# An attention and soft mixture-of-experts kernel: the w2 of expert 5 loaded whole, joins by single copies, and a first output batch stored in two parts

## The chip, the cores and the metric

The kernel runs on one core of one Trainium2 chip. The metric is the device time of an execution in microseconds (us); the median of several runs is compared. Times inside an execution come from one profiled execution and count from the start of its span.

## The reference

Attention with 8 batches, 8 heads, 576 positions and head size 64 is followed by a soft mixture of experts over all 4,608 rows. Four heads see a window of 32 positions, the other four every fourth position of a window of 128. The output of attention is `x` (4608 x 512).

```
logits = x @ phi                                  # 4608 x 32 slots
d = softmax of logits over the rows               # dispatch
slot_input = (d.T @ x).reshape(8, 4, 512)         # 8 experts, 4 slots each
h = np.maximum(slot_input[e] @ w1[e], 0.0)        # 4 x 1024
slot_out[e] = h @ w2[e]                           # 4 x 512
c = softmax of logits over the slots              # combine
out = c @ slot_out                                # 4608 x 512
```

All inputs and the output are float32 in HBM. The kernel computes in fp16 with float32 sums; its DMAs convert on the way.

## The kernel before, in words

**Attention** (lines 445 to 551) runs over the 8 batches as a pipeline of four stages whose order is written out by hand (`ORDER`, line 48); the scheduler keeps the program order on every engine (line 445). ET holds exp(logits) with the slots on partitions, U the sum of d.T @ x.

**Weights.** All loads, and all stores of the output, are issued by GpSimd (POOL), in program order and into one DMA queue. w1 of all experts and w2 of experts 0 to 2 are loaded during attention. When the buffers of the raw inputs are free, lines 536 to 547 load the rest: w2 of experts 3 and 4 whole (1,024 KB as fp16, one DMA each, line 201); then, for the left 256 columns (`s = 0`) and after them for the right 256 (`s = 1`), w2 of experts 5, 6 and 7. Each such half goes as two DMAs of 256 KB (lines 205 to 207). A DMA uses one of eight semaphores in turn, so each issue also waits until the DMA eight before it has landed.

**Slots** (lines 563 to 613). `rs` takes the row sums; `si` holds the slot inputs of the two halves of heads on 64 partitions. Lines 576 to 586 transpose it to `siT` in PSUM, per half `k` with two transposes, and copy it into the block-diagonal `siTm` (half 0 by DVE, half 1 by ACT). Line 596 multiplies by w1 of all experts (64 matmuls), lines 603 to 613 apply the maximum with zero and bring the result, transposed, into `hTm`.

**Second product and join** (lines 621 to 648). `emit_so(s, experts)` adds the products with w2 into `so` in PSUM, eight matmuls for each expert, over all 512 columns (`s` is None) or one half of them. The rows of `so` hold partial sums in four groups. `gather_so(s)` copies a half of the columns to SBUF (`so_part`), and `spread_so(s)` multiplies it by a matrix of ones that adds the groups and repeats the result for them (`rep`), and copies that to `so_sb`. Each of these copies is done in two parts of 128 columns, one by DVE and one by ACT (`part_cols`).

**Output** (lines 652 to 703). `emit_fin` makes one tile of 128 rows: a matmul of ET with `so_sb` (L654), then the scaling by the row's sum, which is also the eviction from PSUM, by ACT (L663) and DVE (L667) in turn. `emit_batch` makes four of them and stores them with one DMA (L674). The order (lines 679 to 698) is: products of experts 0 to 4 over all columns, left products of 5, 6 and 7, left join; then the left half of six batches, with right products put in before the third (expert 5), the fourth (6) and the sixth (7); the right gather before the sixth and the right spread after it; the right half of these six batches; batches 6 and 7 over all columns; and the last 64 rows of every batch (`om_l`, two stores, L701). Left batch, right batch, left store and so on are counted from 0 where they carry a number; the first right store is R0.

Of the kernel before, what the change touches and what calls it, by code (L numbers as in the profile page):

```python
# [9 lines left out]
FP32 = mybir.dt.float32  # L10
FP16 = mybir.dt.float16
# [6 lines left out]
S = 576  # L18
# [7 lines left out]
E_EXP = 8  # L26
S_PER_E = 4
N_SLOTS = 32
# [12 lines left out]
DH = DMODEL // 2  # L41
# [55 lines left out]
def kernel(  # L97
# [10 lines left out]
    nc = tc.nc  # L108
# [9 lines left out]
    ident = cst[:, o : o + 128]  # L118
    spread = cst[:, o + 128 : o + 256]
# [7 lines left out]
    si = consts.tile([64, 4 * D], FP16, name="si")  # L127
    siTm = consts.tile([128, 4, E_EXP, N_SLOTS], FP16, name="siTm")
    rrow = consts.tile([128, NFIN], FP32, name="rrow")
    so_part = consts.tile([128, DMODEL], FP16, name="so_part")  # L130
    so_sb = consts.tile([128, DMODEL], FP16, name="so_sb")
# [19 lines left out]
    def slab_weights(e, tag, n):  # L151
        t = fix.tile([128, n], FP16, name=f"w2_{e}", tag=tag)
        w2t[e] = t[:, 0 : 8 * DMODEL].rearrange("p (c n) -> p c n", c=8)
# [9 lines left out]
    ring = ctx.enter_context(tc.tile_pool(name="ring", bufs=2, space=bass.MemoryType.PSUM))  # L163
# [34 lines left out]
    def load_w2(e, s=None):  # L198
        src = moe_w2[e].rearrange("(p c) n -> p c n", p=128)
        if s is None:  # L200
            nc.gpsimd.dma_start(
                out=w2t[e].rearrange("p c n -> p (c n)"), in_=src.rearrange("p c n -> p (c n)")
            )
            return
        cols = slice(DH * s, DH * s + DH)
        for u in range(2):
            nc.gpsimd.dma_start(out=w2t[e][:, 4 * u : 4 * u + 4, cols], in_=src[:, 4 * u : 4 * u + 4, cols])  # L207
# [162 lines left out]
    def et_cols(b):  # L370
        base = 384 * (b // 2)
        return (base, base + 128) if b % 2 == 0 else (base + 256, base + 192)
# [84 lines left out]
    for which in "QK":  # L457
        load_raw(which, 1)
    nc.gpsimd.dma_start(
        out=phi_raw.rearrange("p (u c) s -> p u (c s)", u=2),  # L460
        in_=moe_phi.rearrange("(u p c) s -> p u (c s)", u=2, c=2),
# [52 lines left out]
    def loads(which, b):  # L514
        load_raw(which, b)
        if which == "V":
            if b > 2:
                load_weights(1)
            if b == B - 1:
                load_weights(len(weights))  # L520
# [6 lines left out]
    for it in range(B + max(s for _, s in STEPS)):  # L527
        for op, stage in STEPS:
            b = it - stage
            if not 0 <= b < B:  # L530
                continue
            step(op, b)
            if op in frees and b + 2 < B:
                loads(frees[op], b + 2)
            left.discard((op, b))
            if w2b_pool is None and not left:
                raw_pool.release()
                w2b_pool = tc.alloc_tile_pool(name="w2b", bufs=1, side="right")
                for e in (3, 4, 5):
                    w2t[e] = w2b_pool.tile([128, 8, DMODEL], FP16, name=f"w2_{e}", tag=f"w2_{e}")  # L540
                slab_weights(6, "qk0", QK_SLAB)
                slab_weights(7, "qk1", QK_SLAB)
                for e in (3, 4):
                    load_w2(e)
                for s in range(2):
                    for e in (5, 6, 7):
                        load_w2(e, s)
        if it == 0:
            nc.vector.tensor_copy(
                out=phi4, in_=phi_raw[:, :, None, :].broadcast_to([128, 4, 4, N_SLOTS])  # L550
            )
# [21 lines left out]
        )  # L573
    nc.vector.reciprocal(out=rcol, in_=U[:, 4 * D : 4 * D + 1])
    nc.vector.tensor_scalar(out=si, in0=U[:, 0 : 4 * D], scalar1=rcol, scalar2=None, op0=ALU.mult)
    for k, copy in enumerate((nc.vector.tensor_copy, nc.scalar.copy)):
        siT = ring.tile([128, 2, N_SLOTS], FP16, name=f"siT{k}", tag="ring")
        rows = slice(32 * k, 32 * k + 32)
        for c in range(2):
            nc.tensor.transpose(siT[:, c, :], si[rows, 128 * c : 128 * c + 128], ident[rows, rows])  # L580
        diag = bass.AP(
            siTm.tensor,
            siTm.offset + 2 * k * E_EXP * N_SLOTS,
            [siTm.ap[0], (E_EXP * N_SLOTS, 2), (N_SLOTS + S_PER_E, E_EXP), (1, S_PER_E)],
        )
        copy(out=diag, in_=siT.rearrange("p c (e s) -> p c e s", e=E_EXP))
    nc.vector.reciprocal(out=rrow, in_=rs)
    hps = psum_e.tile([128, 2, 512], FP32, name="hps", tag="hps")
    h_sb = h_pool.tile([128, FDIM], FP16, name="h_sb", tag="h_sb")
# [1 line left out]
    for fc in range(2):  # L591
        for g in range(2):
            for dc in range(4):
                for j in range(4):
                    e = 4 * g + j
# [4 lines left out]
                        start=(g == 0 and dc == 0),  # L600
                        stop=(g == 1 and dc == 3),
# [3 lines left out]
    for c in range(8):  # L605
# [3 lines left out]
        out=hTm[:, 0].rearrange("p c (j s) -> p c j s", j=4)[:, :, :, 0:16], in_=hT4[:, :, :, 0:16]  # L609
    )  # L610
    nc.scalar.copy(
        out=hTm[:, 1].rearrange("p c (j s) -> p c j s", j=4)[:, :, :, 16:32], in_=hT4[:, :, :, 16:32]
# [4 lines left out]
    om = [w1_pool.tile([128, 4, DMODEL], FP16, name=f"om_{b}", tag=f"w1_{b}") for b in range(B)]  # L617
    om_l = h_pool.tile([128, B // 2, DMODEL], FP16, name="om_l", tag="om_l")
    so = psum_so.tile([128, DMODEL], FP32, name="so", tag="so")

    def emit_so(s, experts):
        cols = slice(0, DMODEL) if s is None else slice(DH * s, DH * s + DH)
        for c in range(8):
            for e in experts:
                g, j = divmod(e, 4)
                row = 32 * (j if len(experts) == 4 else c % 4)
                nc.tensor.matmul(
                    so[row : row + 32, cols],
                    hTm[:, g, c, 32 * j : 32 * j + 32],
                    w2t[e][:, c, cols],  # L630
                    start=(e < 4 and c == 0),
                    stop=(e == 7 and c > 3),
                    skip_group_check=True,
                )

    def part_cols(s):
        c0 = DH * s
        return (nc.vector.tensor_copy, c0), (nc.scalar.copy, c0 + DH // 2)

    def gather_so(s):  # L640
        for copy, c0 in part_cols(s):
            copy(out=so_part[:, c0 : c0 + DH // 2], in_=so[:, c0 : c0 + DH // 2])

    def spread_so(s):
        for copy, c0 in part_cols(s):
            rep = ring.tile([128, DH // 2], FP32, name=f"rep_{c0}", tag="ring")
            nc.tensor.matmul(rep, spread, so_part[:, c0 : c0 + DH // 2], start=True, stop=True)
            copy(out=so_sb[:, c0 : c0 + DH // 2], in_=rep)

    turn = [0]  # L650

    def emit_fin(m, j, c0, c1, dst, blk):
        fp = psum_f.tile([128, DMODEL], FP32, name=f"f_{blk}_{c0}", tag="f")
        nc.tensor.matmul(  # L654
            fp[:, 0 : c1 - c0],
            ET[32 * j : 32 * j + 32, m : m + 128],
            so_sb[32 * j : 32 * j + 32, c0:c1],
            start=True,
            stop=True,
        )  # L660
        turn[0] += 1
        if turn[0] % 2:
            nc.scalar.activation(  # L663
                out=dst, in_=fp[:, 0 : c1 - c0], func=AF.Copy, scale=rrow[:, blk : blk + 1]
            )
        else:
            nc.vector.tensor_scalar(  # L667
                out=dst, in0=fp[:, 0 : c1 - c0], scalar1=rrow[:, blk : blk + 1], scalar2=None, op0=ALU.mult
            )

    def emit_batch(b, c0, c1):
        for j in range(4):
            emit_fin(et_cols(b)[0], j, c0, c1, om[b][:, j, c0:c1], 4 * b + j)
        nc.gpsimd.dma_start(  # L674
            out=out[S * b : S * b + 512].rearrange("(j p) d -> p j d", p=128)[:, :, c0:c1],
            in_=om[b][:, :, c0:c1],
        )

    NHALF = 6
    emit_so(None, (0, 1, 2, 3))  # L680
    emit_so(None, (4,))
    for e in (5, 6, 7):
        emit_so(0, (e,))
    gather_so(0)
    spread_so(0)
    for b in range(NHALF):
        if b in (2, 3, 5):
            emit_so(1, ({2: 5, 3: 6, 5: 7}[b],))
        if b == 5:
            gather_so(1)  # L690
        emit_batch(b, 0, DH)
    spread_so(1)
    for b in range(NHALF):
        emit_batch(b, DH, DMODEL)
    for b in range(NHALF, B):
        emit_batch(b, 0, DMODEL)
# [3 lines left out]
    for e in range(2):  # L700
        nc.gpsimd.dma_start(  # L701
            out=rest[:, e, 512:576, :].rearrange("n i d -> i n d"), in_=om_l[64 * e : 64 * e + 64]
# [37 lines left out]
```

## Time and profile before

| | |
|---|---|
| median of 3 runs | 179.4 us (179.09 to 179.44) |
| the profiled execution | 179.36 us, of which the span has 177.5 |
| busy: PE, DVE, ACT, POOL | 122.4 (69%), 126.3 (71%), 123.8 (70%), 44.5 us (25%) |
| moved by DMA | 40.85 MB by the bytes written, mean 230 GB/s |
| HBM read, written | 62.07 MB, 9.44 MB |
| w2 or w1 DMA of 1,024 KB, of 256 KB: issue to landing | 24.3 us, 15.8 us |
| output DMA of 512 KB: issue to landing | 5.9 us |

The engines are PE (matmul), PEld (its weight loads), DVE, ACT, POOL and SP. The span is cut into 40 slices of 4.44 us; a digit is the busy share of a slice in tenths. In the view of busy times by stretch, each row has the stretch and its length, the busy time and number of instructions of PE, PEld, DVE, ACT and POOL, then the granted share of PE's clock, the time that DMA packets took (over 16 engines; packets of one engine overlap), and GB/s. In the timeline a row has the start, the duration, the engine, the line, the operation and its operands, and in brackets the idle time before and what ended it. `x1` counts instructions. Of every DMA the trace also has 16 landings, one for each of the 16 DMA engines that it is spread over.

### The profile page before, as it was taken

Reading aid. Unit: us, or ns where it says so; the run is one execution under the profiler, and the core shown is the slowest. Engines: PE = TensorE matmul, PEld = TensorE weight load, DVE = VectorE, ACT = ScalarE, POOL = GpSimd, SP = SyncE. Lnnn points to the kernel's source line nnn. Section 1 sums busy time; section 2 is a strip of 40 time slices with the busy share of each in tenths; the row PEclk is TensorE's granted clock in tenths of the full one; section 3 lists DMA queues with packets and bytes.
Section 4 is the critical chain, followed back from the end, with each engine's and each line's share of the span. In section 5 each row is a group of like instructions: output and inputs, shape, how many; then the busy total and the mean of one; then the engine's idle time right before and its main releaser. Section 6 shows DMA issues by size and latency. Waiting matters only on the chain.

```text
span 177.5 us, 4765 instructions
## 1 busy us (share of the span) xinstructions
PE 122.4 (69%) x2016; PEld 79.8 (45%) x2016; DVE 126.3 (71%) x277; ACT 123.8 (70%) x268; POOL 44.5 (25%) x70
## 2 busy tenths in 40 slices
PE   0026828888888988989888988996776736688100
PEld 0015616656666657666666656764332312221000
DVE  6483999999999999799999998455131017789200
ACT  6007758999999999979999999995401117688100
POOL 7321022112112112118110005111111514556400
PEclk9999999999999997599999999789859975555555
DMA  5999999999999999999999999999999999999995
GB/s 90 211 214 211 214 212 215 215 213 217 214 213 216 212 215 212 212 216 216 216 211 215 214 215 223 211 220 220 209 216 190 196 197 224 387 347 394 405 414 142
DMA packets 21061, 40.85 MB, mean 230 GB/s; under 512 B 1328, under 2 KB 13744, under 8 KB 20400
## 3 DMA queue, kind: packets, MB, share of 16 engines
q0 software_dynamic: 20896, 40.41, 114.8%
q8 instruction: 16, 0.26, 0.5%
q1 hardware_dynamic: 144, 0.14, 0.3%
q14 instruction: 5, 0.04, 0.1%
HBM read 62.07 MB, written 9.44 MB: 403 GB/s over the span
## 4 chain that ended last, share of the span: by engine, by line
DMA 46%; ACT 23%; DVE 9%; PE 9%; POOL 4%; issue 3%; POOLq 0%; DVEq 0%; ACTq 0%
DMA w<-in_moe_w_dram 38%; DMA phi_raw<-in_moe_phi_dram 8%; ACT p L269 5%; ACT vX L240 5%; ACT xp L324 4%; PE f L654 3%; DVE qk L218 3%; DVE vT L218 3%; ACT om L663 2%; ACT xT L363 2%; PE rv L234 2%; ACT xT L365 2%; POOL w L193 2%; PE s L260 2%; ACT xd L324 1%
## 5 line engine op out<-in xcount | busy, mean ns | idle before, releaser
L269 ACT ACTIVATE p<-s 128x1920 f16<-128x1920 f32 (+1 forms) x24 | 44.5, 1854 | 10.3 <-PE s L260 10.2
L260 PE MATMUL s<-qk 32*128 32x128 f16 (+2 forms) x704 | 26.7, 295 | 18.9 <-DVE qk L218 12.0
L240 ACT COPY vX<-rv 128x768 f16<-128x768 f16 (+1 forms) x32 | 27.7, 944 | 1.7 <-PE rv L234 1.7
L324 ACT ACTIVATE xp<-o_P,rc_P 128x64 f16<-128x64 f32 x96 | 26.7, 503 | 2.5 <-DVE rc_P L315 2.5
L303 PEld LDWEIGHTS <-p 128*128 128x128 f16 (+1 forms) x480 | 22.4, 103 | 13.4 <-issue 3.9
L260 PEld LDWEIGHTS <-qk 32*128 32x128 f16 x704 | 17.3, 117 | 22.1 <-DVE qk L218 12.0
L280 DVE TENSOR_TENSOR p<-p,masks 128x1920 f16<-128x1920 f16 (+1 forms) x24 | 25.8, 1085 | 0.3
L218 DVE STREAM_TRANSPOSE qk<-rawQ 128x576 uint32<-128x576 uint32 x16 | 18.8, 1242 | 2.7 <-DMA rawQ<-in_q_dram 2.7
L234 PE MATMUL rv<-cst,vT 128*128 128x128 f16 x176 | 18.2, 250 | 3.1 <-DVE vT L218 1.8
L303 PE MATMUL o_P<-vX,p 128*128 128x65 f16 (+1 forms) x288 | 19.8, 204 | 0.7 <-DVE xd L328 0.2
L218 DVE STREAM_TRANSPOSE qk<-rawK 128x576 uint32<-128x576 uint32 x16 | 19.6, 1235 | 0.4 <-DMA rawK<-in_k_dram 0.4
L218 DVE STREAM_TRANSPOSE vT<-rawV 128x576 uint32<-128x576 uint32 x16 | 19.4, 1224 | 0.4 <-DMA rawV<-in_v_dram 0.4
L234 PEld LDWEIGHTS <-vT 128*128 128x128 f16 x176 | 13.8, 126 | 7.1 <-issue 3.7
L667 DVE TENSOR_SCALAR om<-f,rrow 128x256 f16<-128x256 f32 (+1 forms) x28 | 13.5, 518 | 3.7 <-PE f L654 2.2
L207 POOL DMA_DIRECT2D w<-in_moe_w_dram x12 | 8.9, 748 | 26.3 <-DMA w<-in_moe_w_dram 22.4
L663 ACT ACTIVATE om<-f,rrow 128x256 f16<-128x256 f32 (+1 forms) x28 | 12.8, 503 | 3.1 <-PE f L654 2.4
L654 PE MATMUL f<-so_sb,ET 32*128 32x256 f16 (+1 forms) x60 | 12.0, 420 | 3.8 <-ACT om L663 2.5
L674 POOL DMA_DIRECT2D out_dram<-om x14 | 10.4, 747 | 12.4 <-DVE om L667 7.0
L188 POOL DMA_DIRECT2D rawQ<-in_q_dram x8 | 5.1, 633 | 29.5 <-DVE rc_P L315 18.6
L363 ACT COPY xT<-rp 128x576 f16<-128x576 f16 x16 | 11.3, 876 | 1.1 <-PE rp L344 1.1
L303 PE MATMUL o_D<-vX,p 128*128 128x65 f16 x128 | 10.0, 204 | 2.5 <-DVE xp L328 1.4
L365 ACT COPY xT<-rd 128x576 f16<-128x576 f16 x16 | 10.6, 787 | 0.0
(83 smaller groups left out, 182.5 us busy)
## 6 DMA issues: line engine op xcount, KB each, us to landing
w<-in_moe_w_dram POOLq DMA_DIRECT2D x13, 1024.0 KB, 24.3
out_dram<-om POOLq DMA_DIRECT2D x12, 512.0 KB, 5.9
rawQ<-in_q_dram POOLq DMA_DIRECT2D x8, 576.0 KB, 12.6
rawK<-in_k_dram POOLq DMA_DIRECT2D x8, 576.0 KB, 11.3
rawV<-in_v_dram POOLq DMA_DIRECT2D x8, 576.0 KB, 11.4
w<-in_moe_w_dram POOLq DMA_DIRECT2D x12, 256.0 KB, 15.8
out_dram<-om POOLq DMA_DIRECT2D x2, 1024.0 KB, 8.5
out_dram<-om_l POOLq DMA_DIRECT2D x2, 512.0 KB, 9.1
```

The costliest lines, as they stand in the source:

```text
L218: nc.vector.transpose(out=out_, in_=in_)
L234: nc.tensor.transpose(rg[:, n_t, :, c, :], rows, ident)
L240: copy(out=vX[b % 2][:, t0 : t0 + n, :, 0:D], in_=rg.rearrange("p n h c d -> p n h (c d)"))
L260: nc.tensor.matmul(sps[:, h, c0 : c0 + w], kk, qq, start=(tt == 0), stop=(tt == 1))
L269: return nc.scalar.activation(out=pt, in_=sps[:, :, 0:n], func=AF.Exp, scale=SCALE)
L280: return nc.vector.tensor_tensor(out=pt, in0=pt, in1=m, op=ALU.mult)
L303: nc.tensor.matmul(o[rows, h, :], lhs, rhs, start=(n == 0), stop=(n == len(jobs) - 1), skip_group_check=True,)
L324: nc.scalar.activation(out=dst[:, h], in_=src[:, h], func=AF.Copy, scale=rc[:, h : h + 1])
L363: copy(out=xT_t[b][:, c, :], in_=rg[:, 0:S])
L365: copy(out=xT_t[b][:, 2 + c, :].rearrange("p (i r) -> p i r", r=DIL), in_=rg[:, :, 0:SUB].rearrange("p r i -> p i r"),)
L654: nc.tensor.matmul(fp[:, 0 : c1 - c0], ET[32 * j : 32 * j + 32, m : m + 128], so_sb[32 * j : 32 * j + 32, c0:c1], start=True, stop=True,)
L663: nc.scalar.activation(out=dst, in_=fp[:, 0 : c1 - c0], func=AF.Copy, scale=rrow[:, blk : blk + 1])
```

## The change

- w2 of expert 5 is loaded whole by one DMA, behind those of 3 and 4; only 6 and 7 are still loaded as left and right halves. Its products are made over all columns.
- Right products are put in before the third left batch (expert 6) and the fifth (expert 7). The right gather stays before the sixth left batch and the right spread after it.
- `gather_so` is one DVE copy of 256 columns, and `spread_so` one matmul of 256 and one ACT copy.
- The first left batch is stored in two parts: after two of its four tiles, and after the other two.
- `siT` is one PSUM tile, filled by two transposes of all 64 rows in place of four of 32 rows; the two copies into `siTm` follow.

```diff
-                for e in (3, 4):
+                for e in (3, 4, 5):
                     load_w2(e)
                 for s in range(2):
-                    for e in (5, 6, 7):
+                    for e in (6, 7):
                         load_w2(e, s)
...
+    siT = ring.tile([128, 2, 2, N_SLOTS], FP16, name="siT", tag="ring")
+    for c in range(2):
+        nc.tensor.transpose(
+            siT[:, c].rearrange("p k s -> p (k s)"), si[:, 128 * c : 128 * c + 128], ident[0:64, 0:64]
+        )
     for k, copy in enumerate((nc.vector.tensor_copy, nc.scalar.copy)):
-        siT = ring.tile([128, 2, N_SLOTS], FP16, name=f"siT{k}", tag="ring")
-        rows = slice(32 * k, 32 * k + 32)
-        for c in range(2):
-            nc.tensor.transpose(siT[:, c, :], si[rows, 128 * c : 128 * c + 128], ident[rows, rows])
...
-        copy(out=diag, in_=siT.rearrange("p c (e s) -> p c e s", e=E_EXP))
+        copy(out=diag, in_=siT[:, :, k, :].rearrange("p c (e s) -> p c e s", e=E_EXP))
...
-    def part_cols(s):
-        c0 = DH * s
-        return (nc.vector.tensor_copy, c0), (nc.scalar.copy, c0 + DH // 2)
-
     def gather_so(s):
-        for copy, c0 in part_cols(s):
-            copy(out=so_part[:, c0 : c0 + DH // 2], in_=so[:, c0 : c0 + DH // 2])
+        cols = slice(DH * s, DH * s + DH)
+        nc.vector.tensor_copy(out=so_part[:, cols], in_=so[:, cols])
 
     def spread_so(s):
-        for copy, c0 in part_cols(s):
-            rep = ring.tile([128, DH // 2], FP32, name=f"rep_{c0}", tag="ring")
-            nc.tensor.matmul(rep, spread, so_part[:, c0 : c0 + DH // 2], start=True, stop=True)
-            copy(out=so_sb[:, c0 : c0 + DH // 2], in_=rep)
+        cols = slice(DH * s, DH * s + DH)
+        rep = ring.tile([128, DH], FP32, name=f"rep_{s}", tag="ring")
+        nc.tensor.matmul(rep, spread, so_part[:, cols], start=True, stop=True)
+        nc.scalar.copy(out=so_sb[:, cols], in_=rep)
...
-    def emit_batch(b, c0, c1):
-        for j in range(4):
-            emit_fin(et_cols(b)[0], j, c0, c1, om[b][:, j, c0:c1], 4 * b + j)
-        nc.gpsimd.dma_start(
-            out=out[S * b : S * b + 512].rearrange("(j p) d -> p j d", p=128)[:, :, c0:c1],
-            in_=om[b][:, :, c0:c1],
-        )
+    def emit_batch(b, c0, c1, n=4):
+        dst = out[S * b : S * b + 512].rearrange("(j p) d -> p j d", p=128)
+        for j0 in range(0, 4, n):
+            for j in range(j0, j0 + n):
+                emit_fin(et_cols(b)[0], j, c0, c1, om[b][:, j, c0:c1], 4 * b + j)
+            nc.gpsimd.dma_start(
+                out=dst[:, j0 : j0 + n, c0:c1], in_=om[b][:, j0 : j0 + n, c0:c1]
+            )
...
     emit_so(None, (0, 1, 2, 3))
-    emit_so(None, (4,))
-    for e in (5, 6, 7):
+    for e in (4, 5):
+        emit_so(None, (e,))
+    for e in (6, 7):
         emit_so(0, (e,))
     gather_so(0)
     spread_so(0)
     for b in range(NHALF):
-        if b in (2, 3, 5):
-            emit_so(1, ({2: 5, 3: 6, 5: 7}[b],))
+        if b in (2, 4):
+            emit_so(1, ({2: 6, 4: 7}[b],))
         if b == 5:
             gather_so(1)
-        emit_batch(b, 0, DH)
+        emit_batch(b, 0, DH, 2 if b == 0 else 4)
     spread_so(1)
```

## The prediction

> **What bounds the kernel.** I read the slices of the span first.
>
> ```profile
> DMA  5999999999999999999999999999999999999995
> GB/s 90 211 214 211 214 212 215 215 213 217 214 213 216 212 215 212 212 216 216 216 211 215 214 215 223 211 220 220 209 216 190 196 197 224 387 347 394 405 414 142
> ```
>
> The DMA engines are never idle for a whole slice, while PE, DVE and ACT are nearly empty from slice 30 on. The rate doubles after slice 33 because loads (float32 in, fp16 out) are counted by the bytes written; from there on the kernel stores. The busy times by stretch show two rates of loading and one hole:
>
> ```profile
> 120.00:130.00 10.00, 6.71 (x100) 4.28 (x101) 3.83 (x15) 4.44 (x13) 1.48 (x2) 0.85 1.02 213
> 142.00:148.00 6.00, 2.67 (x26) 1.06 (x25) 1.99 (x6) 2.00 (x6) 0.50 (x2) 0.67 1.45 196
> 152.00:157.00 5.00, 3.23 (x21) 1.16 (x21) 3.30 (x10) 3.32 (x11) 1.92 (x3) 0.50 1.98 399
> 157.00:159.00 2.00, 1.61 (x10) 0.43 (x10) 1.84 (x5) 1.82 (x6) 1.64 (x3) 0.50 1.42 284
> 159.00:166.00 7.00, 5.14 (x17) 0.93 (x16) 5.97 (x10) 5.07 (x9) 4.33 (x7) 0.50 1.97 396
> ```
>
> The last column is GB/s: 213 with whole weights, 196 with the w2 pieces of half width, 399 with stores, and only 284 at 157 to 159. The DMA issues of POOL explain the hole:
>
> ```profile
> 147.97 0.75 POOL L674 DMA_DIRECT2D out_dram<-om  x1 [5.50 <-DVE om L667]
> ...
> 154.41 0.75 POOL L674 DMA_DIRECT2D out_dram<-om  x1 [1.04 <-ACT so_sb L648]
> 157.36 0.76 POOL L674 DMA_DIRECT2D out_dram<-om  x1 [2.21 <-ACT om L663]
> ```
>
> The first right store is issued 2.95 us after the last left one; stores that went before had run out. Its first packet moves at 158.65, which is 0.54 after its issue ends. Is the hole on the path? For that I read the landings: every transfer is spread over 16 DMA engines, and each reports its own share.
>
> ```
> transfer                 first lands   last lands
> w2 expert 3 (whole)         128.65       131.25
> w2 expert 4 (whole)         133.52       136.10
> left pieces, 5 to 7                      137.40 138.73 140.13 141.45 142.74 144.28
> right pieces, 5 to 7                     145.48 146.80 148.10 149.43 150.83 152.16
> (the last: nine engines at 149.58 to 150.94, seven at 151.77 to 152.16)
> left store 5                157.64       160.20
> right store 0               160.38       161.46
> last store                  174.56       176.03 (the one before it: 175.64)
> ```
>
> So there are two groups of engines. Nine run ahead and ran dry in the hole; seven, 2.5 us behind, had work all along: their landings go on every 1.31 us. The page's queue list shows what put them behind:
>
> ```profile
> q8 instruction: 16, 0.26, 0.5%
> ```
>
> Each of these 16 packets is 16 KB and takes about 0.95 us of a single engine; in the landings each one sets one engine 1.0 to 1.3 us back. PE has some 4,050 instructions, one packet per 256. The last came at 161.93 and hit an engine of the nine: from 0.2 behind the first it went to 1.5 behind, kept that, and landed last, at 176.03, 0.39 after the seven and 1.3 after the other eight (174.74). The span ends 1.47 later, the execution has 179.36 (median 179.40). **So the end is DMA time alone: work plus idle time on the engine that was hit last, with the seven 0.39 behind it as the next bound.**
>
> **The change, part by part.** *Whole w2 of expert 5.* Four pieces go (12 half-width issues become 8, lines 205 to 207), one whole issue comes. The 12 pieces took 152.16 - 136.10 = 16.06, 1.34 each, four 5.35; whole transfers land 4.86 apart. Every engine is spared 5.35 - 4.86 = **0.49 us**; zero if the row length has nothing to do with the rate, which the 213 against 196 speaks against.
>
> The Trainium skill, "DMA: Bandwidth & Descriptors" (Anatomy of one DMA), fits a DMA as 2.0 us plus bytes over 436 GB/s; by that alone, as an estimate, the whole load saves three fixed costs, 6 us, the split store adds one, 2, and the sum would be -4. The landings 1.34 apart disagree: transfers queued one behind the other hide a fixed cost.
>
> *But the left half is complete later.* Ahead of it now stand one whole and four pieces: 136.10 + 4.86 + 4 x 1.34 = 146.3, not 144.28. From there to the first store: the products of expert 7 wait for this landing and take 0.41 (L627, four). Gather: one DVE copy of 256 columns; the trace has 0.29 for 128 columns and 0.48 to 0.75 for evictions of 256 and 512, 1.04 ns a column, so 0.42. Spread: one matmul of 256, 0.37 by L654 (128 columns: 0.27). One ACT copy, 0.27 + 128 x 0.83 ns = 0.37. Old join 144.77 to 145.98 = 1.21; new 0.42 + 0.37 + 0.37 and hand-overs of 0.05 = 1.28, +0.07 (bounds: -0.3, if the single copies cost what the old halves did, to +0.3). First eviction from 148.5 (146.44 + 2.02 + 0.07). Half a batch is done at 149.1, not 149.5; its issue starts 0.5 after that, as in the other rows of L674, takes 0.63 (256 rows, as L701), and packets move 0.54 later: **150.8**. The nine have finished loading by then (landings 149.1 to 150.46, 0.49 earlier than before); in the old run stores queued at 149.3 caught them without a gap. So all nine stand idle, the slowest for 0.8 (a landing comes 0.4 after the packets that it ends), and start the stores together. The seven, loading to 151.67, don't notice. Bounds: packets from 150.4 to 151.2.
>
> *Next stores.* Second part: packets from 151.4, in time. Second batch: evicted 0.94 later (150.4), issued 150.93, packets 152.2, when the nine want it at 152.1: +0.12. Then the products of right 6 (landed 149.0, PE there at 149.8, no wait), +1.29 as around L627 before, then 0.94, right 7 (landed 151.67, PE there at 152.2, no wait), 1.29: packets of batches 3 to 6 at 153.5, 154.5, 155.8, 157.0, wanted at 153.5, 154.8, 156.2, 157.5. Each such insertion costs 1.29 - 0.94 = 0.35, and there is one fewer than before. The gather before the sixth batch has 0.42 on DVE, with that batch's two DVE evictions behind it; counted. First right store: evicted 156.8, packets at **158.6**, wanted 158.8: the old hole closes.
>
> *Second DMA of the split store*: 16 small completion packets more, **0.03** by the 1.31 for 512 KB against 2.53 for 1 MB.
>
> *Edits at nothing.* One siT tile, two transposes fewer, copies in parallel: 0.1 to 0.4 earlier at 130.4, but the products of experts 0 to 4 end at 141.15 and wait for w2 until 141.49; without that cover it would be a gain. POOL's issues of later pieces wait for the transfer eight before, 0.28 after its landing; seven are always queued ahead, and the last right piece, issued at 141.3, is wanted at 147.8. SP issues nothing new.
>
> **Sum.** The seven: 175.64 - 0.49 + 0.03 = 175.18. The nine: first packets at 150.8, six left stores of 1.31, 0.12 and 0.03 make 158.8; from there to their last landing the old run took 174.74 - 158.65 = 16.1; that is 174.9, and 176.2 on the engine that the last instruction packet sets 1.3 back. It was 176.03, so +0.17: 179.36 + 0.17, **179.5** (by the median 179.6). Loading ends 0.49 earlier, and the later first store takes it back on the engine that matters. The bounds of the first store, 0.4 each way, give 179.1 to 179.9.
>
> **Rivals.** *The last instruction packet stays away.* The change takes 24 of PE's instructions (8 products, 2 transposes, 2 spreads, each with its weight load). Counted back, each packet came some 3.5 us after PE passed a multiple of 256 less about 85 (spread of the fit: 76 to 96); for the 16th that is about 4,011, and 4,020 will be left. A margin of 9: it comes at some 167, still ahead of the end, or not at all. Without it the seven set the end: 175.18, 0.85 less, **178.5**. For it: the narrow margin; against: the best fit. Chance 0.28, with 178.3 to 178.9.
>
> *The right join is late (slower).* Between the end of R0's evictions and its issue lie 1.74 us, in every other row 0.5; no wait in the trace accounts for 1.25 of it. If this belongs to the join, R0's packets move at 159.9, past the 158.8 from which it decides, and the nine idle 1.1 longer: 179.5 + 1.1, **180.6** (180.0 to 180.9). Against: another cause fits. Up to that store an engine had 1,008 of POOL's packets, with it 1,041 (each transfer's rows over 16 and one for completion; the page's 20,896 are 1,306 per engine). If the stall belongs to the 1,024th packet, it moves: the change removes 122, and the fifth right store crosses it, wanted at 164.0 and even 1.25 late there at 163.7. The Trainium skill has such a size: "SBUF — State Buffer" (SBUF size) gives 16 KiB per partition to the descriptor rings, "DMA: Bandwidth & Descriptors" (Terms) 16 B to a descriptor, by estimate 1,024; no page states a stall. Chance of the late join 0.14.
>
> *The whole load isn't faster*: 0.49 comes back, **180.0**; chance 0.05, the rates speak against it.
>
> **How the numbers follow.** Forecast 0.48 (179.1 to 179.9), no packet 0.28, late join 0.14, no faster load 0.05, others 0.05. About 0.2%, 0.36 us, is what a measurement here can tell from no change: below 179.04 faster, above 179.76 slower. The forecast gives 0.07 to faster, 0.29 to same, 0.12 to slower; no packet 0.27 to faster; late join and slow load 0.18 to slower; others in thirds. Faster 0.36, same 0.32, slower 0.32. For 8 in 10 the range goes from 178.4 (no packet) to 180.4 (a late join in part); the likeliest case alone is 179.1 to 179.9.
>
> **What would show it.** The last w2 piece landing last at 151.7; last left piece at 146.3; the first store issued at 149.6 and a dip of GB/s at 149 to 151 in place of that at 157 to 159; 15 or 16 packets on q8; the 1.25 us stall at the fifth right store or at the first; the engine landing last alone by 0.9 (forecast) or with six others. Wrong if loading doesn't end earlier, if packets of the first store move before 150.4 or after 151.2, or if PE waits for right 6 or 7.

## The result and the profile after

The changed kernel takes 178.56 us (median of 6, 178.43 to 178.86), the kernel before beside it 179.42 (6 runs); ratio 0.9955, 95% interval 0.9944 to 0.9965. It is 0.86 us faster. Run again on another chip it had 0.9951 (0.9937 to 0.9964). The forecast was no change, 179.5; what was measured is the time that the prediction gave to its first rival, 178.5. The profiled execution after is one of 178.43 us.

The slices of the span and the queue list of the page after, to be laid beside those of before:

```profile
DMA  5999999999999999999999999999999999999997
GB/s 89 210 215 209 216 213 215 214 213 215 215 214 216 214 213 215 213 213 216 213 214 214 217 211 227 209 221 217 213 213 219 192 197 174 326 400 395 402 413 222
...
q8 instruction: 15, 0.25, 0.5%
```

There are 15 instruction packets, not 16 (q8 is the queue that brings them). And there is a dip of GB/s now, 174, in the slice before the stores. The busy times by stretch of the changed kernel place it:

```profile
142.00:148.00 6.00, 1.77 (x17) 0.62 (x17) 0.42 (x1) 0.23 (x1) 0.05 (x1) 0.67 1.45 194
149.00:151.00 2.00, 1.80 (x16) 0.64 (x16) 1.51 (x5) 1.38 (x5) 1.26 (x2) 0.50 0.79 106
152.00:157.00 5.00, 3.52 (x27) 1.22 (x26) 3.97 (x10) 3.89 (x11) 2.98 (x4) 0.50 1.94 395
157.00:159.00 2.00, 1.55 (x7) 0.41 (x7) 1.56 (x5) 1.83 (x6) 1.49 (x2) 0.50 1.98 396
```

The hole at 157 to 159 (284 GB/s before) has gone; at 149 to 151 there is a deeper one, 106 GB/s: the nine engines that have finished loading wait for the first store. POOL's part of the timeline shows when it came, and where POOL was held up later:

```profile
149.74 2.18 POOL L673 DMA_DIRECT2D out_dram<-om  x3 [7.68 <-DVE om L664]
...
157.11 0.74 POOL L673 DMA_DIRECT2D out_dram<-om  x1 [0.68 <-ACT om L660]
...
160.43 0.74 POOL L673 DMA_DIRECT2D out_dram<-om  x1 [0.22 <-ACT om L660]
162.69 2.22 POOL L673 DMA_DIRECT2D out_dram<-om  x3 [1.52 <-ACT om L660]
```

The first row holds both parts of the first store and the second batch. The store at 157.11 is the first right one; it follows the left ones without the 2.95 us of before. The gap of 2.26 us between two issues is now ahead of the fifth right store, at 162.69.

The two profiled executions differ by 0.93 us. Of this 0.16 lies behind the last landing: from there to the end of the span it is 1.47 us before and 1.31 after. No run tested what sets these 0.16; the end takes 1.30 and 1.31 too in the two kernels below that get the packet back, so it isn't the packet.

### The profile page after: what moved, and what is told of

It reads as the page before. It is cut to its first block, busy times and chain, and to the rows that moved or that the text cites. A ratio compares the mean times of both kernels' runs of the same rounds, so it can differ in the third digit from the quotient of the medians.

```text
span 176.7 us, 4735 instructions
## 1 busy us (share of the span) xinstructions
PE 123.1 (70%) x2004; PEld 80.0 (45%) x2004; DVE 126.0 (71%) x275; ACT 123.3 (70%) x266; POOL 42.6 (24%) x68
## 4 chain that ended last, share of the span: by engine, by line
DMA 50%; DVE 27%; PE 7%; issue 5%; ACT 4%; POOL 3%; POOLq 0%
DMA w<-in_moe_w_dram 34%; DVE qk L218 10%; DMA phi_raw<-in_moe_phi_dram 8%; DMA rawQ<-in_q_dram 8%; DVE vT L218 5%; DVE p L280 5%; PE f L651 5%; ACT om L660 3%; DVE xd L328 2%; DVE xp L328 1%; PE so L628 1%; POOL rawQ L188 1%; DVE om_l L664 1%; PE s L260 1%; POOL rawV L188 1%
## 5 line engine op out<-in xcount | busy, mean ns | idle before, releaser
L324 ACT ACTIVATE xp<-o_P,rc_P 128x64 f16<-128x64 f32 x96 | 26.1, 482 | 2.2 <-DVE rc_P L315 2.2
L234 PE MATMUL rv<-cst,vT 128*128 128x128 f16 x176 | 17.6, 242 | 3.2 <-DVE vT L218 1.8
L234 PEld LDWEIGHTS <-vT 128*128 128x128 f16 x176 | 13.1, 124 | 7.6 <-issue 3.7
L651 PE MATMUL f<-so_sb,ET 32*128 32x256 f16 (+1 forms) x60 | 12.5, 418 | 4.1 <-ACT om L660 2.9
L673 POOL DMA_DIRECT2D out_dram<-om x15 | 11.1, 742 | 13.2 <-DVE om L664 8.3
L207 POOL DMA_DIRECT2D w<-in_moe_w_dram x8 | 5.9, 743 | 29.2 <-DMA w<-in_moe_w_dram 28.6
```

The lines of the kernel that those rows point to most:

```text
L234: nc.tensor.transpose(rg[:, n_t, :, c, :], rows, ident)
L324: nc.scalar.activation(out=dst[:, h], in_=src[:, h], func=AF.Copy, scale=rc[:, h : h + 1])
L651: nc.tensor.matmul(fp[:, 0 : c1 - c0], ET[32 * j : 32 * j + 32, m : m + 128], so_sb[32 * j : 32 * j + 32, c0:c1], start=True, stop=True,)
```

## The experiments

From the landings and the DMA packets of each profiled execution I took the same few times. "Last w2 after expert 4" is the time from the last landing of expert 4's w2 to that of the last w2 piece; the start of this stretch differs by up to 0.7 us from execution to execution, so differences say more than clock times.

```
kernel                 q8   last w2   first store's   last landing   last landing after
                            after     packets after   of all         the first store's
                            expert 4  expert 4's w2                  packets
before                 16    16.06       13.23          176.03           26.70
changed                15    15.53       14.80          175.35           24.34
changed, again         15    15.52       14.80          175.90           24.35
changed + 12 transp.   16    15.54       14.49          176.26           25.42
changed + 8 transp.    16    15.52       14.79          176.80           25.44
changed, half pieces   15    16.05       15.33          176.66           24.96
changed, one store     15    15.53       15.22          176.10           24.29
changed, old joins     15    15.53       14.75          175.29           24.35
changed, four stores   15    15.55       14.27          175.88           25.22
before, whole w2       15    15.53       15.19          176.06           24.51
before, 12 fewer       15    16.06       13.42          175.61           26.11
before, joins and siT  16    16.05       13.19          175.91           26.56
```

**The theory** was: the end is set by the DMA engine with the most work and idle time; the change takes 0.5 us of loading and, by having 24 PE instructions fewer, one 16 KB instruction packet from it. **The rival**: the packet is of no account, and the shorter loading, the closed hole or the joins bring the gain.

**12 repeated transposes added to the changed kernel** (eight once more, four a third time). 4,034 PE instructions again (2,016 matmuls, as many weight loads, two more). The prediction counted ten rows more in each kernel, waits and a drain that PE's sequencer has in the trace; its 4,020 for the changed kernel is 4,010 here.

```diff
-    for c in range(8):
+    for c in (*range(8), *range(8), *range(4)):
         nc.tensor.transpose(hT[:, c, :], h_sb.rearrange("p (q l) -> p l q", l=8)[:, c, :], ident)
```

> The changed kernel, with 12 of the transposes at L606 done a second time (PE gets its 24 removed instructions back, at a place where it waits for w2 anyway). Theory (the instruction packet): q8 shows 16 packets again, the last near 162 to 164; one engine falls 1.0 to 1.3 us behind the others and lands last, 179.5 to 179.8 us. Rival (the gain is the shorter loading and the closed hole, and the packet hits no engine that matters): 178.6 us whatever q8 shows.

179.76 us, ratio to before 1.0009 (0.9998 to 1.002): the whole gain is gone. The page of this kernel:

```profile
q8 instruction: 16, 0.26, 0.5%
```

The 16th packet came at 162.89. The first store's packets were 0.31 earlier than in the changed kernel, and loading took as long; the difference stands in the last column of the table, 1.08 us, and in the landings of the last store: fifteen engines within 174.80 to 175.42, one at 176.26. Counted from the landing of expert 4's w2, the fifteen are done after 39.1 us, as all sixteen are in the changed kernel; the one engine is 0.84 later. The theory holds, and so does the forecast for the case of 16 packets (179.5).

**8 repeated transposes added.** 4,026 instructions; the same edit without `*range(4)`.

> The changed kernel with 8 of the transposes at L606 done a second time: 4,026 instructions on PE, between 4,018 (15 packets on q8) and 4,034 (16). Theory (the time follows the number of packets, not the extra work): 178.7 us if q8 shows 15 packets, 179.7 us if it shows 16. Rival (the extra work of PE costs in proportion): two thirds of what 12 transposes cost, 179.3 to 179.4 us with either number.

179.53 us, ratio 1.000 (0.9991 to 1.001), 16 packets; last column 25.44, the same as with 12. Fifteen engines are again done 39.1 us after expert 4's w2, and one lands 1.11 later (176.80 against 175.69). So it is the packet and not the work of the added instructions.

**The kernel before without the row sums, 12 matmuls.** 4,010 instructions.

```diff
-    rs = ring.tile([128, NFIN], FP32, name="rs", tag="ring")
-    for b in range(B):
-        m = et_cols(b)[0]
-        nc.tensor.matmul(
-            rs[:, 4 * b : 4 * b + 4], ET[:, m : m + 128], quad, start=True, stop=True
-        )
-    for pr in range(B // 2):
-        l = et_cols(2 * pr)[1]
-        nc.tensor.matmul(
-            rs[:, 4 * B + pr : 4 * B + pr + 1], ET[:, l : l + 128], quad[:, 0:1], start=True, stop=True
-        )
...
-    nc.vector.reciprocal(out=rrow, in_=rs)
+    nc.vector.memset(rrow, 1.0 / 32)
```

> The kernel before without the 12 matmuls that sum the rows (rs); the rows' factor is a constant instead, so the output is not scaled by the sums. Nothing else is changed, and PE has 24 instructions fewer. Theory (the instruction packet): 15 packets on q8, the seven engines set the end, 0.39 us earlier: 179.0 us. Rival (packet of no account): 179.4 us.

179.07 us, ratio 0.9970 (0.9961 to 0.9979), so 0.56 less (0.39 was expected, which the interval still holds); 15 packets. The hole at the first right store is there as before (2.96 us between issues), and the last landing, 175.61, is one of seven between 175.4 and 175.61, no longer of one engine alone. In this kernel the packet is worth less than 1.08, since the engine that it hits was ahead of the seven.

**The kernel before with the whole w2 alone.** Its loads, its products over all columns and no right products of 5; 4,018 instructions.

```diff
-                for e in (3, 4):
+                for e in (3, 4, 5):
...
-                    for e in (5, 6, 7):
+                    for e in (6, 7):
...
-    emit_so(None, (4,))
-    for e in (5, 6, 7):
+    for e in (4, 5):
+        emit_so(None, (e,))
+    for e in (6, 7):
         emit_so(0, (e,))
...
-        if b in (2, 3, 5):
-            emit_so(1, ({2: 5, 3: 6, 5: 7}[b],))
+        if b in (3, 5):
+            emit_so(1, ({3: 6, 5: 7}[b],))
```

> The kernel before with one part of the change alone: w2 of expert 5 whole, its products over all columns (joins, siT, the one store of the first batch and the places of right 6 and 7 as before). PE has 16 instructions fewer. Theory: loading ends 0.49 us earlier; the first store's packets move at about 151.5, so all engines wait for it 0.2 to 0.4 us; with 15 packets on q8 178.8 to 179.0 us, with 16 of them 179.8 to 180.2 us. Rival (the other parts of the change carry the gain): 179.4 us with either number of packets.

179.17 us, ratio 0.9981 (0.9970 to 0.9992), 15 packets: 0.46 less than the kernel before by the medians (179.63 on this chip) and 0.34 by the ratio; 0.4 to 0.6 less was expected (178.8 to 179.0 against 179.4). The first store's packets move 0.39 later after expert 4's w2 than in the changed kernel, and all engines wait for them.

**The changed kernel with w2 of expert 5 in half-width pieces.**

```diff
-                for e in (3, 4, 5):
+                for e in (3, 4):
                     load_w2(e)
+                for s in range(2):
+                    load_w2(5, s)
```

> The changed kernel with w2 of expert 5 loaded as four half-width pieces, at the place of the whole load; all else as changed. Theory (row length sets the rate of loading): the last w2 piece lands 0.49 us later, 179.05 us; if the stall of 1.25 us belongs to the 1,024th packet of an engine, it comes at the first right store again and adds 0.2 to 0.5 us more: 179.3 to 179.5 us. Rival (the whole load saves nothing): 178.6 us and the last piece at 151.7.

180.00 us, ratio 1.0022 (1.0012 to 1.0031), 1.2 us above the changed kernel by the ratios, some 0.3 more than the most that was expected (179.5 against 178.56). Loading takes 16.05 in place of 15.53, as in the kernel before: the whole load saves 0.53. The other 0.6 stands in the last column, and the timeline of POOL in this kernel shows where it comes from:

```profile
156.38 0.75 POOL L675 DMA_DIRECT2D out_dram<-om  x1 [0.37 <-issue]
159.08 3.75 POOL L675 DMA_DIRECT2D out_dram<-om  x5 [1.95 <-ACT om L662]
```

The store at 159.08 is the first right one. The stall is back there, and here the engines have nothing left meanwhile: their last landing for this store comes 2.1 us after that for the store ahead, not 1.33.

**The other parts of the change.** The changed kernel once more, beside three variants on the same chip.

> The changed kernel once more, as the reference of this group: 0.86 us under the kernel before, 15 packets on q8.

178.77 us, ratio 0.9951 (0.9937 to 0.9964), 15 packets.

The first batch stored at once:

```diff
-        emit_batch(b, 0, DH, 2 if b == 0 else 4)
+        emit_batch(b, 0, DH)
```

> The changed kernel with the first left batch stored by one DMA again. Theory (all engines start the stores together, at the first packet of the first store): the first store is issued 0.5 us later, its packets move at 151.5 in place of 151.0, the seven engines too now wait, 0.2 to 0.4 us more than the changed kernel. Rival (the split only adds a DMA): the same or 0.03 us less.

179.02 us, ratio 0.9964 (0.9950 to 0.9978). The first packets are 0.42 later and the last column is 0.05 less; the time is 0.25 above the changed kernel, as expected, but the two intervals overlap, so the size is inconclusive.

The old joins (`part_cols` and the two-part `gather_so` and `spread_so` of before put back):

```diff
+    def part_cols(s):
+        c0 = DH * s
+        return (nc.vector.tensor_copy, c0), (nc.scalar.copy, c0 + DH // 2)
```

> The changed kernel with the joins of the kernel before (two parts of 128 columns, DVE and ACT). PE has 4 instructions more than the changed kernel, 4,014 rows, 15 packets. Theory: the join takes 1.2 us in place of 1.25, nothing else moves: within 0.1 us of the changed kernel. Rival (the single copies are a part of the gain): 0.3 us more or above.

178.52 us, ratio 0.9937 (0.9924 to 0.9950). That is 0.25 below the changed kernel on the same chip, more than the 0.1 expected, but the two intervals overlap, and loading, first store and last column agree with the changed kernel within 0.05. The single copies are not part of the gain; whether they cost anything stays open.

The first batch stored in four parts (`1 if b == 0 else 4`):

> The changed kernel with the first left batch stored in four parts. Theory: the first packets move 0.3 to 0.4 us earlier, which helps only the nine engines that wait for them; the seven set the end, and four issues on POOL push the second batch back by 0.2 to 0.3: within 0.15 us of the changed kernel. Rival (the first packet alone sets the end): 0.3 us less.

178.95 us, ratio 0.9958 (0.9945 to 0.9972): not told apart from the changed kernel. The first packets are 0.53 earlier, the last column is 0.88 more, so the last landing comes 0.35 later after expert 4's w2. The second batch was issued 0.35 later behind the four issues on POOL, where 0.2 to 0.3 was expected.

**The joins and siT alone, in the kernel before.** 4,026 instructions; the functions and the transposes as in the change.

```diff
+    siT = ring.tile([128, 2, 2, N_SLOTS], FP16, name="siT", tag="ring")
...
+        nc.tensor.matmul(rep, spread, so_part[:, cols], start=True, stop=True)
+        nc.scalar.copy(out=so_sb[:, cols], in_=rep)
```

> The kernel before with the single-copy joins and the one siT tile alone: loads, products, their places and the store of the first batch as before. 4,026 instructions on PE. Theory: with 16 packets on q8 the same as the kernel before, within 0.1 us; with 15 of them 0.4 to 0.5 us less. Rival (the joins are worth something by themselves): less by 0.3 us or more with 16 packets too.

179.19 us, ratio 0.9989 (0.9979 to 0.9999), 16 packets: 0.28 less by the medians and 0.2 by the ratio, where at most 0.1 was expected. The last engine landed 0.21 after the next one, in the kernel before 0.39, so a part of it may be how far ahead the engine was that the packet hit. The interval reaches from nothing to 0.4, so the rival (0.3 or more by the joins themselves) is not excluded here; against it stands the run with the old joins, which lost nothing.

## Why the prediction was wrong, point by point

**What bounds the kernel** was right. In all twelve profiled executions the span ends 1.3 to 1.5 us after the last landing of a store, and the transposes that were added to PE left the other fifteen engines where they had been.

**The whole load** was given 0.49 and measured 0.53 (16.06 against 15.53; with half pieces in the changed kernel 16.05). The rule of the Trainium skill weighed there ("DMA: Bandwidth & Descriptors", Anatomy of one DMA), 2.0 us fixed for each DMA, would by estimate have made loading 6 us longer with half pieces. The traces disagree: it got 0.53 longer.

**The later left half and the first store** were right step by step. In the timeline of the changed kernel, the products of expert 7, the one-copy gather, the one spread and the one copy:

```profile
146.43 0.41 PE L628 MATMUL so<-w,hTm 128*32 128x256 f16 x4 [0.89 <-DMA w<-in_moe_w_dram]
...
146.88 0.42 DVE L639 CAST so_part<-so 128x256 f16<-128x256 f32 x1 [8.77 <-PE so L628]
147.36 0.37 PE L644 MATMUL rep<-so_part,cst 128*128 128x256 f16 x1 [0.53 <-DVE so_part L639]
...
147.76 0.37 ACT L645 CAST so_sb<-rep 128x256 f16<-128x256 f32 x1 [9.03 <-PE rep L644]
148.19 0.40 PE L651 MATMUL f<-so_sb,ET 32*128 32x256 f16 x4 [0.46 <-ACT so_sb L645]
```

0.42, 0.37 and 0.37 were forecast for the three; the left half landed at 146.4 (146.3), the first store was issued at 149.74 (149.6), its packets moved at 151.0 (150.8). No wait for right 6 or 7 is seen, and the hole at the first right store closed.

**The last instruction packet is the step that failed.** The prediction let it come, at 1.3 us on the engine that lands last, and gave 0.28 to its staying away. Its ground was the place of PE at which the earlier packets had come: about 85 rows ahead of a multiple of 256, so for the 16th row 4,011, with 4,020 rows left. That place held where a 16th packet came: in the four kernels that have one it came 3.0 to 3.3 us after PE began row 4,011. The step from there was wrong, that reaching the place brings the packet. In the changed kernel PE began row 4,011 at 163.67, in all eight executions with 15 packets between 162.66 and 164.37, over 11 us ahead of the last landing, and no packet came. What the runs show in its place is that the length of the program decides: 4,010, 4,014 and 4,018 instructions had 15 packets, 4,026 and 4,034 had 16 (in the prediction's rows 4,020 to 4,028 against 4,036 and 4,044). That fits a packet being fetched only when the program reaches into it: 16 times 256 is 4,096, so 70 to 78 instructions that this count leaves out would have to stand in the program too. This reading was not tested further. The price of the packet was about right: 0.85 on the time was forecast, 0.8 to 1.0 measured.

**The sum for the case that came** was right too: the seven were to end at 175.18 and the nine at 174.9, and all sixteen ended within 174.96 to 175.35; 178.5 was given, 178.56 measured. That the two groups came out nearly level is one difference: the first store's packets moved 0.2 later than forecast, and the nine wait for them. That 178.5 was met so closely is in part luck: the last landing was 0.17 later than in this sum, and the end of the span behind it 0.16 shorter. The second DMA of the split store was given 0.03; its own numbers, twice 1.31 against 2.53, give up to 0.09, and the run with one store had 0.05 less in the last column.

**The late right join** did not come, for the reason given against it. The stall of POOL follows the count of packets per engine: with some 1,000 of them ahead of the first right store it stands there (the kernel before, without row sums, with new joins alone, and the changed one with half pieces), and with 886 ahead, or near it, at the fifth right store (the other eight). So in all twelve it stands where an engine's count passes some number between 1,020 and 1,041. It cost nothing in the changed kernel and 0.6 us in the one with half pieces. Why POOL stalls there was not tested. The sizes that the Trainium skill gives ("SBUF — State Buffer", SBUF size, and "DMA: Bandwidth & Descriptors", Terms), by which I estimated 1,024 descriptors for a ring, agree with this.

## What to carry to other kernels

When the DMA engines bound a kernel, read the landings of each engine, not the mean: here the last 0.4 us belonged to one engine out of sixteen, and what set it back was the code of PE. A kernel whose instruction count lies just above the point at which one more packet is fetched (here between 4,018 and 4,026 instructions of PE) may gain about as much from a dozen instructions fewer as from a better load, and an edit that adds a few can lose it. And ask of a gain which of its accidents carried it: with the packet put back, the five edits together were worth nothing that these runs can tell, and the kernel before gained 0.56 of the 0.86 without any of them, when 12 of its matmuls were left out and with them the packet.

## What the runs showed of the hardware that was not expected

An instruction packet is 16 KB, takes about 0.95 us, and sets back one DMA engine: in the two kernels that got it back, that engine landed 0.84 and 1.11 us behind the other fifteen. Whether the 16th is fetched changed between 4,018 and 4,026 PE instructions. Rows of 512 B as written load at 1.34 us for 256 KB, whole rows at 4.86 for 1,024 KB. And POOL's issue was held once in each execution, 1.8 to 1.9 us behind the last eviction in place of 0.5, at the store with which an engine's count of packets of that queue passes some number between 1,020 and 1,041.
